# Accumulators of one PSUM bank each in the seven-product stage of an attention and feed-forward kernel

## The chip, the cores and the metric

The kernel runs on one core of a Trainium2 chip. The metric is device time in microseconds of one execution, given as the median of several runs. Engines are named as in the profile: PE (matmul), PEld (weight load), DVE (vector), ACT (scalar), POOL (GpSimd), SP (which issues the output transfers).

## The reference

Block-sparse attention over (4, 8, 768, 64) inputs, then a feed-forward layer over the 3072 tokens:

```python
k_sum = k.reshape(B, H, nb, block, D).max(axis=3)      # block 32
v_sum = v.reshape(B, H, nb, block, D).mean(axis=3)
# each query: keys closer than 16, and the 24 block summaries; softmax over both
x = attn_out.transpose(0, 2, 1, 3).reshape(B * S, H * D)   # 3072 x 512
h = x @ w_in                                               # 512 -> 2048
g = h * (1.0 / (1.0 + np.exp(-beta * h)))
return g @ w_out                                           # 2048 -> 512
```

## The kernel before

The work is cut by batch. Attention of the next batch runs beside the feed-forward layer of the current one; a list of steps with hand-written due times (`run(main, side)`) sets the order in which the instructions are written, and every engine executes its own in that order. Semaphores between the engines are placed by the tile framework: an instruction waits for the earlier instructions that touch the same tile and conflict with it.

The feed-forward layer of one batch has an up part (`h_group`: matmuls into `h_ps`, then a SiLU on ACT into `h_sb`) and a down part. For the first three batches the down part is plain (`o_part`, `o_piece`). For the last batch alone it is done by `down_seven`. There the 768 x 2048 by 2048 x 512 product is treated as a 2 x 2 block matrix product (two halves of tokens, of the 2048 inner columns, and of the 512 output columns) and computed with seven block products in place of eight, as Strassen does. Sums of blocks are formed ahead by DVE (`sums_w`, `sums_h`). This stage is the end of the kernel: nothing but the output transfers comes behind it.

`down_seven` works on three row groups a, b and c (`ms` = 0, 1, 2), each 128 tokens of either half. A product, say a6, is product 6 of group a: eight matmuls of 128 x 256 into half a bank (L690). Each group has three accumulator banks:

- `x` holds products 3 (with 6 added later) and 4,
- `y` holds products 5 and 2,
- `z` holds product 1 (with 7 added later).

Group by group, these readers follow:

- `low_copy` (ACT, L695) copies `y` to SBUF as `o_low`;
- `cross` (DVE, L700 and L701) reads `x` twice;
- `minus` (DVE, L707) reads product 1 in `z`;
- `end(6)` (DVE, L712) reads `x` after product 6 was added, `end(7)` (L712) reads `z` after product 7 was added, and each has SP issue an output transfer (L715). For the last group `cross` issues two transfers as well (L703, L704).

The products of the three groups are written in this order, with the readers behind some of them:

a3 a4 a2 a5 (`a.low_copy`) a1 (`a.cross`, `a.minus`) b3 b4 a6 (`a.end(6)`) a7 (`a.end(7)`) b2 b5 (`b.low_copy`) b1 (`b.cross`, `b.minus`) c5 c2 (`c.low_copy`) c3 c4 (`c.cross`) b6 (`b.end(6)`) b7 (`b.end(7)`) c1 (`c.minus`) c6 (`c.end(6)`) c7 (`c.end(7)`)

PSUM has eight banks. Two are buffers of the small pool (tag `t`); six belong to a pool that can be re-cut: `cut(n)` closes it and opens it anew as 6/n buffers of n banks, and `take(name)` takes the next one. Before the change it stands at n = 2 here. Banks `x` and `z` of a group are the two halves of one tile `o_big`, and `y` is a tile `o_ps` of the small pool.

Of the kernel before, what the change touches and what calls it, by code (L numbers as in the profile page):

```python
# [12 lines left out]
def kernel(  # L13
# [12 lines left out]
    P = 128  # L26
    f32 = mybir.dt.float32
# [19 lines left out]
    d_model = moe_w_in.shape[0]  # L47
# [21 lines left out]
    ps = ctx.enter_context(tc.tile_pool(name="ps", bufs=1, space=bass.MemoryType.PSUM))  # L69
# [209 lines left out]
    def cut(n):  # L279
        if "ctx" in pools:  # L280
            pools.pop("ctx").close()
        pools["ctx"] = ExitStack()
        pools["n"] = n
        pools["pool"] = pools["ctx"].enter_context(tc.tile_pool(name=f"banks{n}", bufs=1, space=bass.MemoryType.PSUM))

    def take(name, dt=f32):
        n = pools["n"]
        return pools["pool"].tile([P, n, 512 if dt == f32 else 1024], dt, name=name, tag="big", bufs=6 // n)
# [383 lines left out]
    class Seven:  # L672
# [2 lines left out]
        def __init__(self, u, ms):  # L675
            self.u, self.ms, self.row = u, ms, units[u][0] * nch + units[u][1] // P + ms

        def open(self):
            big = take("o_big")
            low = ps.tile([P, d_model], f32, name="o_ps", tag="t", bufs=2)  # L680
            n = d_model // 2
            self.x, self.y, self.z, self.n = big[:, 0], low, big[:, 1], n
            self.at = {3: big[:, 0, 0:n], 4: big[:, 0, n:], 5: low[:, 0:n], 2: low[:, n:], 1: big[:, 1, 0:n]}
            self.at[6], self.at[7] = self.at[3], self.at[1]

        def dots(self, *ms):
# [30 lines left out]
    def down_seven(u, add):  # L717
        a, b, c = (Seven(u, ms) for ms in range(HM))
        c.last = u + 1 == len(units)

        def each(z, m, *then):
            def f():
                if m == z.first:
                    z.open()
                z.dots(m)
                for g in then:
                    g()
            add(f)

        for z in (a, b):  # L730
            z.first = 3
        c.first = 5
        for m in (3, 4, 2):
            each(a, m)
        each(a, 5, a.low_copy)
        each(a, 1, a.cross, a.minus)
        each(b, 3)
        each(b, 4)
        each(a, 6, lambda: a.end(6))
        each(a, 7, lambda: a.end(7))  # L740
        each(b, 2)
        each(b, 5, b.low_copy)
        each(b, 1, b.cross, b.minus)
        each(c, 5)
        each(c, 2, c.low_copy)
        each(c, 3)
        each(c, 4, c.cross)
        each(b, 6, lambda: b.end(6))
        each(b, 7, lambda: b.end(7))
        each(c, 1, c.minus)  # L750
        each(c, 6, lambda: c.end(6))
        each(c, 7, lambda: c.end(7))
# [189 lines left out]
    for b in range(B):  # L942
# [6 lines left out]
        main, t = [], 0.0  # L949
# [24 lines left out]
        for u in us_rest:  # L974
            if u in seven:
                def add(f):
                    nonlocal_t[0] = nonlocal_t[0] + OT
                    main.append((nonlocal_t[0] - OT, f))
                nonlocal_t = [t]
                down_seven(u, add)  # L980
                t = nonlocal_t[0]
                continue
            for ms in range(units[u][2] * HM):
                for p in range(4):
                    main.append((t, lambda u=u, ms=ms, p=p: o_part(u, ms, p, 4)))
                    t += OT
# [4 lines left out]
        if b == 0:  # L991
# [23 lines left out]
            for g in pairs:  # L1015
                t = dn0 + OT * TK[g] if g < 2 else up1 + TK[g]
# [15 lines left out]
        elif nxt < B:  # L1032
            for g in pairs:
                t = (2.6, 6.5, 10.4, 14.3)[g]
# [69 lines left out]
```

## Time and profile before

| | |
|---|---|
| median of 3 runs | 211.62 us (211.50 to 212.26) |
| the profiled execution | 213.69 us |
| its span, first to last instruction | 212.0 us |
| PE busy | 202.8 us, 96% |
| DVE busy | 125.7 us, 59% |
| ACT busy | 119.8 us, 57% |
| POOL busy | 83.5 us, 39% |
| mean granted clock of PE | 0.992 |

Times in the trace count from the start of the span. A row of the timeline gives start, time, engine, line, operation, what is written and read, shapes, and the number of instructions merged into the row; in square brackets stands how long the engine had been idle before, and who ended that. Matmuls are pipelined: each of this stage is shown with about 272 ns, while they start closer together than that, so a row of eight ends later than the next row starts.

### The profile page before, as it was taken

What the parts mean: (1) busy time and instruction counts of PE and PEld (TensorE: products, weight loads), DVE (VectorE), ACT (ScalarE), POOL (GpSimd) and SP (SyncE); (2) the same over time, 40 slices, a digit from 0 to 9 for tenths busy, and PEclk for the clock granted to TensorE, in tenths of its full rate; (3) what the DMA queues carried; (4) which work ended last, traced back from release to release, by engine and by line L of the source; (5) the groups of instructions that cost most, each with busy time, mean ns of one, the idle gap of its engine ahead of it and who ended that gap; (6) DMA issues with size and microseconds to landing.
All of it is one profiled execution on the core that took longest, in us unless ns stands there. A gap on an engine that the chain in (4) does not pass through costs nothing.

```text
span 212.0 us, 5108 instructions
## 1 busy us (share of the span) xinstructions
PE 202.8 (96%) x2100; PEld 119.9 (57%) x2100; DVE 125.7 (59%) x339; ACT 119.8 (57%) x172; POOL 83.5 (39%) x122
## 2 busy tenths in 40 slices
PE   7897999999999999999999999999999999999972
PEld 2565655556545555655555456655555566587861
DVE  4884948988969869434626669814435444443341
ACT  3682889159797386668336266678164276631200
POOL 7996999793055399984300094000000000000000
PEclk9996999999999999999999999999999999999999
DMA  6999999999939999999992999900343400000141
GB/s 153 180 156 207 200 205 204 188 151 218 140 62 146 114 202 139 156 163 156 159 216 92 111 179 156 167 13 0 118 108 91 136 2 3 0 0 34 68 148 50
DMA packets 92199, 26.46 MB, mean 125 GB/s; under 512 B 81152, under 2 KB 89360, under 8 KB 92176
## 3 DMA queue, kind: packets, MB, share of 16 engines
q0 software_dynamic: 63888, 13.34, 76.1%
q1 hardware_dynamic: 28080, 12.60, 31.2%
q8 instruction: 16, 0.26, 0.6%
q10 hardware_dynamic: 208, 0.20, 0.3%
q14 instruction: 7, 0.06, 0.1%
HBM read 27.27 MB, written 6.29 MB: 158 GB/s over the span
## 4 chain that ended last, share of the span: by engine, by line
PE 91%; DMA 3%; DVE 2%; issue 2%; POOL 1%; ACT 0%; ACTq 0%
PE h_ps L619 36%; PE o_ps L789 25%; PE o_big L690 5%; PE o_ps L804 5%; PE h_ps L768 4%; DMA q<-in_q_dram 3%; PE av_ps L572 3%; PE o_ps L690 2%; PE s_ps L527 2%; PE px L493 1%; PE s_ps L510 1%; DVE o_two L712 1%; PE vm_ps L376 1%; PE pq L310 1%; PE vm_ps L386 1%
## 5 line engine op out<-in xcount | busy, mean ns | idle before, releaser
L619 PE MATMUL h_ps<-xT,w_in_sb 128*128 128x384 bf16 x464 | 77.1, 327 | 0.0
L632 ACT ACTIVATE h_sb<-h_ps,beta_sb 128x768 bf16<-128x768 f32 (+1 forms) x80 | 59.2, 775 | 23.2 <-PE h_ps L619 19.3
L619 PEld LDWEIGHTS <-w_in_sb 128*128 128x128 bf16 x464 | 45.2, 98 | 30.0 <-issue 0.3
L789 PE MATMUL o_ps<-w_out_sb,h_sb 128*128 128x512 bf16 x240 | 54.9, 380 | 0.0
L789 PEld LDWEIGHTS <-h_sb 128*128 128x128 bf16 x240 | 22.3, 98 | 25.0
L553 DVE TENSOR_TENSOR attn<-attn,band 128x768 bf16<-128x768 bf16 x24 | 13.0, 556 | 18.9 <-ACT attn L502 17.2
L792 ACT COPY o_sb<-o_ps 128x512 f32<-128x512 f32 x15 | 8.9, 596 | 22.3 <-PE o_ps L789 17.1
L112 POOL DMA_DIRECT2D q_all<-in_q_dram x24 | 20.3, 873 | 2.7 <-DMA ve<-in_v_dram 2.7
L502 ACT ACTIVATE attn<-s_ps 128x768 bf16<-128x768 f32 x24 | 17.7, 814 | 3.3 <-PE s_ps L527 2.2
L118 POOL DMA_DIRECT2D ve<-in_v_dram x16 | 16.6, 1051 | 1.8 <-DMA w_out_sb<-in_moe_w_out_dram 1.1
L112 POOL DMA_DIRECT2D k_all<-in_k_dram x16 | 13.9, 883 | 2.8 <-DMA ve<-in_v_dram 2.0
L348 DVE TENSOR_TENSOR half<-kw 128x384 bf16<-128x384 bf16 x16 | 5.8, 365 | 10.8 <-DMA kw<-k_all 10.7
L582 DVE TENSOR_TENSOR x_nat<-av_ps,r 128x768 bf16<-128x768 f32 x12 | 11.5, 958 | 0.5
L690 PEld LDWEIGHTS <-h_sb 128*128 128x128 bf16 x96 | 9.4, 97 | 4.2 <-issue 3.0
L804 PE MATMUL o_ps<-w_out_sb,h_sb 128*128 128x512 bf16 x48 | 11.7, 380 | 0.0
L369 DVE COPY vo<-ve 64x780 bf16<-64x780 bf16 (+3 forms) x28 | 10.6, 380 | 0.6
L665 DVE TENSOR_TENSOR ve<-h_sb 128x768 bf16<-128x768 bf16 x4 | 2.2, 558 | 13.2 <-ACT h_sb L632 13.2
L246 ACT ACT_TABLE_LOAD x7 | 9.0, 1283 | 0.1
L690 PE MATMUL o_big<-w_sum,h_sb 128*128 128x256 bf16 x48 | 6.2, 272 | 2.3 <-DVE o_two L712 1.8
L768 PE MATMUL h_ps<-xT,w_in_sb 128*128 128x384 bf16 x48 | 8.3, 326 | 0.0
L495 ACT COPY xT<-px 128x384 bf16<-128x384 bf16 (+1 forms) x5 | 3.0, 607 | 9.0 <-PE px L493 9.0
L695 ACT COPY o_low<-o_ps 128x512 f32<-128x512 f32 x3 | 1.8, 586 | 10.9 <-PE o_ps L690 10.9
(142 smaller groups left out, 252.8 us busy)
## 6 DMA issues: line engine op xcount, KB each, us to landing
out_dram<-o_sb SPq DMA_DIRECT2D x18, 256.0 KB, 3.1
ve<-in_v_dram POOLq DMA_DIRECT2D x12, 192.0 KB, 6.4
q_all<-in_q_dram POOLq DMA_DIRECT2D x24, 96.0 KB, 6.2
w_in_sb<-in_moe_w_in_dram POOLq DMA_DIRECT2D x8, 256.0 KB, 8.8
k_all<-in_k_dram POOLq DMA_DIRECT2D x16, 96.0 KB, 6.5
w_out_sb<-in_moe_w_out_dram POOLq DMA_DIRECT2D x4, 256.0 KB, 7.0
w_out_sb<-in_moe_w_out_dram POOLq DMA_DIRECT2D x2, 512.0 KB, 9.2
out_dram<-o_two SPq DMA_DIRECT2D x4, 256.0 KB, 2.3
```

The source lines that it names most:

```text
L112: nc.gpsimd.dma_start(out=t[:, :, h], in_=(k_row if nm == "k" else q_row)[b, g, :, h])
L118: nc.gpsimd.dma_start(out=ve_bufs[b % 2][:, lo:hi, 0:D], in_=src)
L369: copy(out=dst, in_=src)
L502: nc.scalar.activation(out=at[(b, g)][:, par].rearrange("p m h f -> p h m f"), in_=sv, func=ACTF.Exp, scale=scale)
L553: nc.vector.tensor_mul(out=a, in0=a, in1=band[:, par])
L582: nc.vector.tensor_mul(out=x.rearrange("p m h d -> p h m d"), in0=ov[:, :, :, 0:D], in1=r[:, :, :, None].to_broadcast([P, 2, n, D]))
L619: nc.tensor.matmul(big[:, j, 0:MG], w_in_sb[:, ki, ni * P:(ni + 1) * P], xT[b][:, ki, tok:tok + MG], start=(ki == 0), stop=(ki == k1 - 1))
L632: nc.scalar.activation(out=hb.rearrange("p (k m) -> p k m", m=MG), in_=big[:, j:j + w, 0:MG], func=ACTF.Silu, scale=beta_sb[:, ni:ni + 1])
L690: nc.tensor.matmul(self.at[m], h[:, c, self.ms * P:(self.ms + 1) * P], w[:, c], start=(c == 0 and m in (1, 3, 2 if self.first == 3 else 5) ...
L768: nc.tensor.matmul(h_open[(u, i)][:, j, 0:MG], w_in_sb[:, ki, ni * P:(ni + 1) * P], xT[b][:, ki, t0 + j * MG:t0 + (j + 1) * MG], start=sta ...
L789: nc.tensor.matmul(o_ps, h_bufs[(u, ni * w // k2)][:, ni % (k2 // w), ms * P:(ms + 1) * P], w_out_sb[:, ni], start=(ni == 0), stop=(ni == ...
L804: nc.tensor.matmul(o_ps, h_bufs[(u, ni * w // k2)][:, ni % (k2 // w), ms * P:(ms + 1) * P], w_out_sb[:, ni], start=(ni == 0), stop=(ni == ...
```

## The change

Each of the accumulators `x`, `y` and `z` becomes a tile of its own, of one bank. At the start of `down_seven`, group a takes both buffers of the small pool as `x` and `y`; the other pool is re-cut into six single banks; a takes one of them as `z`, b takes three, c takes two and uses a's `y` again. The tiles of the re-cut pool are called `o_one`. Lines move up by one from `dots` on: L690 becomes L689, L695 L694, L700 L699, L701 L700, L707 L706, L712 L711, L715 L714.

```diff
-        def open(self):
-            big = take("o_big")
-            low = ps.tile([P, d_model], f32, name="o_ps", tag="t", bufs=2)
+        def open(self, banks):
             n = d_model // 2
-            self.x, self.y, self.z, self.n = big[:, 0], low, big[:, 1], n
-            self.at = {3: big[:, 0, 0:n], 4: big[:, 0, n:], 5: low[:, 0:n], 2: low[:, n:], 1: big[:, 1, 0:n]}
+            x, y, z = banks
+            self.x, self.y, self.n = x, y, n
+            self.at = {3: x[:, 0:n], 4: x[:, n:], 5: y[:, 0:n], 2: y[:, n:], 1: z[:, 0:n]}
             self.at[6], self.at[7] = self.at[3], self.at[1]
...
     def down_seven(u, add):
         a, b, c = (Seven(u, ms) for ms in range(HM))
         c.last = u + 1 == len(units)
+        low = []
+
+        def banks(z):
+            if z is a:
+                low.extend(ps.tile([P, d_model], f32, name="o_ps", tag="t", bufs=2) for _ in range(2))
+                cut(1)
+                return low[0], low[1], take("o_one")[:, 0]
+            if z is b:
+                return tuple(take("o_one")[:, 0] for _ in range(3))
+            return take("o_one")[:, 0], low[1], take("o_one")[:, 0]
 
         def each(z, m, *then):
             def f():
                 if m == z.first:
-                    z.open()
+                    z.open(banks(z))
                 z.dots(m)
```

On PE at the passage from product c1 to c6, near the end of the program, this stands before (`h_sum` is the left operand of product 1, `h_sb` of product 6; the number behind a name tells buffers apart; in brackets, the engine for whose semaphore the instruction waits):

```order
L690 LDWEIGHTS h_sum_1570
L690 MATMUL o_big_3132<-w_sum_1567,h_sum_1570 128x256
L690 LDWEIGHTS h_sb_2850
L690 MATMUL o_big_3132<-w_sum_1567,h_sb_2850 128x256 [waits DVE_49]
L690 LDWEIGHTS h_sb_2850
```

And now, at the same place on PE:

```order
L689 LDWEIGHTS h_sum_1570
L689 MATMUL o_one_3139<-w_sum_1567,h_sum_1570 128x256
L689 LDWEIGHTS h_sb_2850
L689 MATMUL o_one_3138<-w_sum_1567,h_sb_2850 128x256 [waits DVE_49]
L689 LDWEIGHTS h_sb_2850
```

Nothing moved; both products wrote one tile before and write two now. The first matmul of c6 still waits for DVE, but for an earlier instruction of it: the last one that reads `x`.

On DVE the last seven instructions of the stage were these (`c.cross` twice, `b.end(6)` and `b.end(7)` in one row, `c.minus`, `c.end(6)`, `c.end(7)`; names as above, `o_two` is the output tile in SBUF):

```order
L700 TENSOR_TENSOR o_two_3167<-o_big_3132,o_low0_1568 128x512 [waits DMAHW4_49,DMAHW5_49,PE_49,Activation_49]
L701 TENSOR_TENSOR o_low0_1568<-o_big_3132,o_low0_1568 128x256 [waits DVE_49]
L712 TENSOR_TENSOR o_two_3128<-o_big_3065,o_low1_1569 128x256 [waits PE_49] x2
L707 TENSOR_TENSOR o_low0_1568<-o_big_3132,o_low0_1568 128x256 [waits PE_49]
L712 TENSOR_TENSOR o_two_3167<-o_big_3132,o_low0_1568 128x256 [waits DVE_49,PE_49]
L712 TENSOR_TENSOR o_two_3167<-o_big_3132,o_low0_1568 128x256 [waits PE_49]
```

and now they are these:

```order
L699 TENSOR_TENSOR o_two_3173<-o_one_3138,o_low0_1568 128x512 [waits DMAHW4_49,DMAHW5_49,PE_49,Activation_49]
L700 TENSOR_TENSOR o_low0_1568<-o_one_3138,o_low0_1568 128x256 [waits DVE_49]
L711 TENSOR_TENSOR o_two_3134<-o_one_3070,o_low1_1569 128x256 [waits PE_49]
L711 TENSOR_TENSOR o_two_3134<-o_one_3072,o_low1_1569 128x256 [waits PE_49]
L706 TENSOR_TENSOR o_low0_1568<-o_one_3139,o_low0_1568 128x256 [waits PE_49]
L711 TENSOR_TENSOR o_two_3173<-o_one_3138,o_low0_1568 128x256 [waits DVE_49,PE_49]
L711 TENSOR_TENSOR o_two_3173<-o_one_3139,o_low0_1568 128x256 [waits PE_49]
```

The order of the DVE instructions is the same, and each reads a tile of one bank.

## The prediction

> **What bounds the kernel now.** I read the page first, then the waits of the last 25 us, then that stretch in order of time on PE and DVE, and last the output transfers and the clock. The page gives the span and the chain that ended last:
>
> ```profile
> span 212.0 us, 5108 instructions
> PE 91%; DMA 3%; DVE 2%; issue 2%; POOL 1%; ACT 0%; ACTq 0%
> ```
>
> PE carries the chain almost everywhere, so time is only to be had where PE stands still. The change touches nothing ahead of the block products, which start at 187.11 us; I take everything before that as unchanged. In the waits from 187 to 212 us (total, times, longest), PE has two rows:
>
> ```profile
> PE o_big L690 <- DVE o_two L712: 1.8, 3, 0.8
> PE o_big L690 <- DVE o_low L707: 0.5, 1, 0.5
> ```
>
> PE waits four times for a DVE instruction that reads the accumulator. The timeline of PE (start, time, idle before) shows where. Each x8 is one product, each x16 two:
>
> ```profile
> 187.11 1.91 PE L690 MATMUL o_big<-w_out_sb,h_sb 128*128 128x256 bf16 x16
> ...
> 191.48 1.91 PE L690 MATMUL o_big<-w_out_sb,h_sb 128*128 128x256 bf16 x16
> 193.29 1.03 PE L690 MATMUL o_big<-w_sum,h_sb 128*128 128x256 bf16 x8
> 194.83 1.03 PE L690 MATMUL o_big<-w_sum,h_sb 128*128 128x256 bf16 x8 [0.51 <-DVE o_two L712]
> 195.70 1.04 PE L690 MATMUL o_ps<-w_out_sb,ve 128*128 128x256 bf16 x8
> ...
> 200.07 1.91 PE L690 MATMUL o_big<-w_out_sb,h_sb 128*128 128x256 bf16 x16
> 201.82 1.04 PE L690 MATMUL o_big<-w_sum,h_sb 128*128 128x256 bf16 x8
> 203.61 1.03 PE L690 MATMUL o_big<-w_sum,h_sb 128*128 128x256 bf16 x8 [0.75 <-DVE o_two L712]
> 204.48 1.04 PE L690 MATMUL o_big<-w_sum,h_sum 128*128 128x256 bf16 x8
> 206.03 1.03 PE L690 MATMUL o_big<-w_sum,h_sb 128*128 128x256 bf16 x8 [0.51 <-DVE o_low L707]
> 207.58 1.03 PE L690 MATMUL o_big<-w_sum,h_sb 128*128 128x256 bf16 x8 [0.52 <-DVE o_two L712]
> ```
>
> By the order in the code, 193.29 is a6 (row group a, product 6), 194.83 a7, 201.82 b6, 203.61 b7, 204.48 c1, 206.03 c6, 207.58 c7. The idle in brackets understates the loss, because a matmul's modelled end lies beyond the start of the next one. The loss is better read from starts. From 194.83 to 201.82 there are eight products without a stop: 6.99 / 8 = 0.874 us each. That is the pace that PE can hold here.
>
> The DVE timeline says what PE waited for:
>
> ```profile
> 192.48 0.42 DVE L701 TENSOR_TENSOR o_low<-o_big,o_low 128x256 f32<-128x256 f32 x1
> 192.82 0.41 DVE L707 TENSOR_TENSOR o_low<-o_big,o_low 128x256 f32<-128x256 f32 x1
> 194.36 0.42 DVE L712 TENSOR_TENSOR o_two<-o_big,o_low 128x256 f32<-128x256 f32 x1 [1.12 <-PE o_big L690]
> ...
> 202.07 0.69 DVE L700 TENSOR_TENSOR o_two<-o_big,o_low 128x512 f32<-128x512 f32 x1 [2.00 <-issue]
> 202.80 0.42 DVE L701 TENSOR_TENSOR o_low<-o_big,o_low 128x256 f32<-128x256 f32 x1
> 203.14 0.41 DVE L712 TENSOR_TENSOR o_two<-o_big,o_low 128x256 f32<-128x256 f32 x1
> 204.68 0.42 DVE L712 TENSOR_TENSOR o_two<-o_big,o_low 128x256 f32<-128x256 f32 x1 [1.12 <-PE o_big L690]
> 205.55 0.42 DVE L707 TENSOR_TENSOR o_low<-o_big,o_low 128x256 f32<-128x256 f32 x1 [0.45 <-PE o_big L690]
> 207.10 0.42 DVE L712 TENSOR_TENSOR o_two<-o_big,o_low 128x256 f32<-128x256 f32 x1 [1.12 <-PE o_big L690]
> 208.65 0.42 DVE L712 TENSOR_TENSOR o_two<-o_big,o_low 128x256 f32<-128x256 f32 x1 [1.12 <-PE o_big L690]
> ```
>
> a7 (194.83) starts 0.05 us after `a.end(6)` has read product 6 (194.36 + 0.42 = 194.78). But a7 writes `big[:, 1]` and `a.end(6)` reads `big[:, 0]`; they share the tile, not the bank. So with b7 behind `b.end(6)` (203.14 + 0.41 = 203.55), and c7 behind `c.end(6)` (207.52). c6 writes `big[:, 0]` and waits for `c.minus` (205.97), which reads `big[:, 1]`. All four waits come from a tile that is larger than what is read or written.
>
> **The change part by part.** One tile per bank leaves each matmul waiting for the readers of its own bank alone. What that is worth, from the starts:
>
> - a6: two products from 191.48 to 193.29 take 1.81, at pace 1.75; lost 0.06. Before, a6 is behind `a.minus` (192.82 + 0.41 = 193.23). After, it needs only `a.cross`, whose L701 ended at 192.90 in this trace and can only be earlier.
> - a7: 194.83 − 193.29 = 1.54, less 0.874: 0.67. After, it needs `a.minus`, done some 0.9 us before a7 is due at 194.10.
> - b7: 203.61 − 201.82 = 1.79, less 0.874: 0.92. It is the dearest since DVE was in `c.cross` when product 6 came. After, it needs `b.minus`, which follows b1, five products earlier.
> - c6: 206.03 − 204.48 = 1.55, less 0.874: 0.68. After, it needs `c.cross` alone.
> - c7: 207.58 − 206.03 = 1.55: 0.68. After, it needs `c.minus`, and this one is close (below).
>
> Sum: 0.06 + 0.67 + 0.92 + 0.68 + 0.68 = 3.01 us.
>
> Does a new wait take their place? I laid out PE at 0.874 a product: a6 193.23, a7 194.10, then b2, b5, b1, c5, c2, c3, c4 at 200.22, b6 201.09, b7 201.97, c1 202.84, c6 203.72, c7 204.59. A reader starts 1.07 us after the first matmul of its product (207.58 to 208.65). `c.cross` came 1.12 after c4 (second half of the x16 at 200.07, so 200.95, to 202.07): now 201.34, its second step 202.07, then `b.end(6)` at 202.41, `b.end(7)` at 203.04, `c.minus` at 202.84 + 1.07 = 203.91. DVE has gaps between all of these, so its order stays harmless. `c.minus` ends at 204.33; with 0.06 to PE (205.97 to 206.03) c7 could start at 204.39 and is due at 204.59. Cover: 0.20 us. If it is gone, c7 waits by what is missing, at most the 0.68 that it waits now. c6 needs the end of `c.cross`, 202.07 + 0.42 = 202.49, and is due 1.2 us later.
>
> The rest costs nothing. There are as many matmuls, DVE passes, ACT copies and output DMAs as before, in the same order. Group a's first two banks now come from the small pool, the other six from the pool that is re-cut to single banks; its first use is a1, four products after the start, so at about 190.6. The last reader of an `h_ps` bank on ACT ends at 188.21:
>
> ```profile
> 187.31 0.90 ACT L632 ACTIVATE h_sb<-h_ps,beta_sb 128x768 bf16<-128x768 f32 x1 [0.40 <-PE h_ps L619]
> ```
>
> Group c reuses a's bank `y`, as it reused the same buffer before; between a5, after which ACT copies it, and c5 stand eight products, 7 us. A loss from six single-bank buffers filling up is excluded, since a, b and c together take six.
>
> Behind the last matmul come `c.end(7)` on DVE, its DMA issued by SP and the landing. The output transfers now come closer together. SP's issues, the traffic in half-microsecond windows (PE, PEld, DVE, ACT, POOL busy, clock, DMA share, GB/s) and the landing of the `o_two` transfers:
>
> ```profile
> 202.79 0.33 SPq L703 DMA_DIRECT2D out_dram<-o_two  x1
> ...
> 209.10 0.33 SPq L715 DMA_DIRECT2D out_dram<-o_two  x1
> 203.50:204.00 0.50, 0.39 (x4) 0.35 (x4) 0.05 (x1) 0.00 (x0) 0.00 (x0) 1.00 0.69 234
> 204.00:204.50 0.50, 0.50 (x7) 0.44 (x6) 0.00 (x0) 0.00 (x0) 0.00 (x0) 1.00 0.80 268
> 204.50:205.00 0.50, 0.50 (x7) 0.46 (x5) 0.32 (x1) 0.00 (x0) 0.00 (x0) 1.00 0.84 318
> 205.00:205.50 0.50, 0.50 (x5) 0.31 (x4) 0.10 (x1) 0.00 (x0) 0.00 (x0) 1.00 0.61 230
> DMA to landing us min/median/max: 1.7/1.9/3.5
> ```
>
> Bytes flow some 0.7 us after the issue, at a mean of 262 GB/s over these four windows. After the change, `c.cross`'s two transfers of 128 KB and b's two of 256 KB are issued from 202.06 to about 203.5: 0.79 MB, 3.0 us at that rate, so done near 205.8. `c.end(6)` is issued at about 205.25 and its bytes flow from 205.95. So the last two transfers should find a free queue. Bounds: 0, and 3.5 − 1.7 = 1.8 us if the last landing becomes the longest seen. I take 0, since the row is that of a clear queue.
>
> With that, the last reader starts at 204.59 + 1.07 = 205.66 in place of 208.65, its DMA at 206.11 in place of 209.10, and the span ends near 209.0. The profiled execution took 213.69 us, so it would take about 210.7. It is 2.07 us above the median of 211.62, with no sign that this part differs, so I subtract the same 3.01 from the median: **208.6 us**, 1.4% faster.
>
> The Trainium skill, TensorE: Matmul & The Clock Gate, section Back-to-back issue gap, would have it better still: it gives for streams of weight load and matmul about 81 ns each at 128 columns and 131 ns at 512. Between these an estimate for 256 columns is 98 ns, by which the 14 products from a6 on would end 14 × 8 × (109 − 98) = 1.2 us earlier and the sum come to 207.4. The trace does not agree: 0.874 / 8 = 109 ns with nothing in the way, and the measurement decides.
>
> **The rivals.** First, *one wait stays*: c7 behind `c.minus`, with only 0.20 us of cover, or another reader that comes late. It gives back up to 0.68, or 0.92 where it is b7: 209.3 to 209.5. Against it: the steps of 1.07, 0.42 and 0.06 repeat to 0.01 us in the rows.
>
> Second, *the end is handed to the transfers*: landing 1.8 us longer, 210.4. For it: 0.79 MB in 1.5 us of issues, twice as dense as now. Against it: the reckoning above.
>
> Third, *the change does not do what it says*, because PE waits for something other than the shared tile: 211.6, no change. Against it: nothing that DVE writes in these microseconds is read by a7, b7, c6 or c7, so only the accumulator can order them.
>
> Fourth, on the other side, *the clock drops* in a stage that no longer pauses. The windows (columns as above) show that it can drop in this kernel:
>
> ```profile
> 18.00:21.00 3.00, 3.00 (x43) 2.48 (x37) 1.80 (x6) 1.16 (x4) 2.63 (x6) 0.50 1.24 204
> 187.00:193.00 6.00, 6.00 (x56) 5.34 (x55) 3.65 (x8) 1.49 (x2) 0.00 (x0) 1.00 0.00 0
> 203.00:208.00 5.00, 3.36 (x28) 2.72 (x28) 1.83 (x5) 0.00 (x0) 0.00 (x0) 1.00 0.43 157
> ```
>
> At 0.50, 18:21 us loses half of its 3 us, 1.5 us. The gain of 3.0 and the 1.06 us that make 0.5% are gone after 8.1 us at half clock: 212.7 at that point. Against it: the clock was 1.00 both in the six microseconds without a pause and in the five with three pauses. The Trainium skill, same page, section A second HAM failure mode: psum-queue depth-cycling, says that a kernel which cycles through PSUM banks can idle PE so briefly and often that the clock swings between half and full. This change cycles through more single banks; no run so far shows such a swing here, and the four pauses in this trace, which would be its cause, did not set it off.
>
> **How the numbers follow.** Forecast 0.85; one wait stays 0.06; transfers 0.04; no effect 0.03; clock 0.02. What this kernel's measurement can tell from no change is about 0.5%, 1.06 us. Below 210.56 lie the forecast, the one wait and half of the transfers' case: faster 0.93. Same: 0.02 + 0.03 = 0.05. Slower: 0.02. The range's upper end, 209.8, takes in the kept wait (209.5) and a part of a longer landing. The lower, 208.0, is the lowest run (211.50) less 3.01, less 0.5 for the spread of the runs, which was 0.76 from lowest to highest.
>
> **What would show it.** In the profile after, the groups of 8 from 187.11 on should start 0.87 us apart throughout, with no idle before a PE row named after DVE, and the waits of PE on L711 and L706 should be gone; the last DVE read should start near 205.7, `b.end(6)` and `b.end(7)` near 202.4 and 203.0, the span should end near 209.0. A gap before the last x8 would mean that the 0.20 us of cover was not there. A last landing above 2 us would be the transfers; a clock under 1.00 after 187 us the fourth rival. I would be wrong by the whole sum if the four gaps stood where they are.

## The result

The changed kernel took 209.65 us (median of 4 runs, 209.32 to 209.89) beside 211.9 us for the kernel before (4 runs): ratio 0.9893, 95% interval 0.9867 to 0.9919, 2.25 us faster. Measured again on one chip, five runs against 23 of the kernel before, it was 209.29 beside 212.13 us: ratio 0.9864, interval 0.9842 to 0.9885, 2.84 us faster. The forecast was 208.6 us and 3.01 us of gain. In microseconds the first interval is 1.7 to 2.8 and stops short of 3.01; the second, 2.4 to 3.4, holds it.

The chain that ended last, by engine, in the profile after (span 207.6 us, profiled execution 209.32 us), is PE for 96% of the span, where it was 91%:

```profile
span 207.6 us, 5089 instructions
PE 96%; issue 1%; ACT 1%; DVE 0%
```

The PE timeline of the stage after, with the columns of the prediction's:

```profile
185.76 1.91 PE L689 MATMUL o_ps<-w_out_sb,h_sb 128*128 128x256 bf16 x16
...
190.13 1.91 PE L689 MATMUL o_one<-w_out_sb,h_sb 128*128 128x256 bf16 x16
191.87 1.04 PE L689 MATMUL o_ps<-w_sum,h_sb 128*128 128x256 bf16 x8
192.75 1.04 PE L689 MATMUL o_one<-w_sum,h_sb 128*128 128x256 bf16 x8
193.62 1.04 PE L689 MATMUL o_one<-w_out_sb,ve 128*128 128x256 bf16 x8
...
199.73 1.91 PE L689 MATMUL o_one<-w_sum,h_sb 128*128 128x256 bf16 x16
201.48 1.04 PE L689 MATMUL o_one<-w_sum,h_sum 128*128 128x256 bf16 x8
202.35 1.91 PE L689 MATMUL o_one<-w_sum,h_sb 128*128 128x256 bf16 x16
```

No row has an idle in brackets. a6 (191.87) to a7 (192.75) is 0.88, b6 and b7 stand in one row of 16, and so do c6 and c7. The 20 products up to c7 keep the pace of 0.874. On DVE, `b.end(6)`, `b.end(7)`, `c.minus`, `c.end(6)` and `c.end(7)` now are:

```profile
201.06 0.41 DVE L711 TENSOR_TENSOR o_two<-o_one,o_low 128x256 f32<-128x256 f32 x1
201.68 0.42 DVE L711 TENSOR_TENSOR o_two<-o_one,o_low 128x256 f32<-128x256 f32 x1 [0.21 <-PE o_one L689]
202.56 0.42 DVE L706 TENSOR_TENSOR o_low<-o_one,o_low 128x256 f32<-128x256 f32 x1 [0.45 <-PE o_one L689]
203.43 0.42 DVE L711 TENSOR_TENSOR o_two<-o_one,o_low 128x256 f32<-128x256 f32 x1 [0.45 <-PE o_one L689]
204.30 0.42 DVE L711 TENSOR_TENSOR o_two<-o_one,o_low 128x256 f32<-128x256 f32 x1 [0.45 <-PE o_one L689]
```

DVE now waits for PE before each of the last three, by the same 0.45 us, and PE for nobody. From a3 to the last read the stage takes 204.30 − 185.76 = 18.54 us, where it took 208.65 − 187.11 = 21.54: 3.00 less. The spans differ by more, 4.4 us, since the two profiled executions also differ ahead of the stage (last section).

### The profile page after: what moved, and what is told of

It reads as the page before. It is cut to its first block, busy times and chain, and to the rows that moved or that the text cites. A ratio compares the mean times of both kernels' runs of the same rounds, so it can differ in the third digit from the quotient of the medians.

```text
span 207.6 us, 5089 instructions
## 1 busy us (share of the span) xinstructions
PE 200.1 (96%) x2082; PEld 119.7 (58%) x2100; DVE 127.4 (61%) x339; ACT 119.7 (58%) x172; POOL 83.2 (40%) x122
## 4 chain that ended last, share of the span: by engine, by line
PE 96%; issue 1%; ACT 1%; DVE 0%
PE h_ps L619 37%; PE o_ps L798 25%; PE o_one L689 6%; PE o_ps L813 5%; PE h_ps L777 4%; PE o_ps L689 3%; PE av_ps L572 3%; PE w_ps L826 3%; PE s_ps L527 2%; PE pk L310 1%; PE s_ps L422 1%; PE s_ps L510 1%; PE pq L310 1%; PE vm_ps L376 1%; PE px L493 1%
## 5 line engine op out<-in xcount | busy, mean ns | idle before, releaser
L632 ACT ACTIVATE h_sb<-h_ps,beta_sb 128x768 bf16<-128x768 f32 (+1 forms) x80 | 59.2, 774 | 23.3 <-PE h_ps L619 19.4
L798 PE MATMUL o_ps<-w_out_sb,h_sb 128*128 128x512 bf16 x226 | 52.3, 379 | 1.7 <-issue 1.4
L502 ACT ACTIVATE attn<-s_ps 128x768 bf16<-128x768 f32 x24 | 17.7, 814 | 3.3 <-PE s_ps L527 2.2
L813 PE MATMUL o_ps<-w_out_sb,h_sb 128*128 128x512 bf16 x44 | 11.5, 380 | 0.2
L689 PEld LDWEIGHTS <-h_sb 128*128 128x128 bf16 x96 | 9.4, 98 | 1.2
L358 DVE COPY kw<-kw 128x192 bf16<-128x192 bf16 (+2 forms) x32 | 8.1, 298 | 0.0
L255 DVE TENSOR_SCALAR w_out_sb<-w_out_sb,inv_beta 128x512 bf16<-128x512 bf16 x16 | 6.6, 464 | 1.9 <-DMA w_out_sb<-in_moe_w_out_dram 1.9
```

What stands on the lines that cost most here:

```text
L502: nc.scalar.activation(out=at[(b, g)][:, par].rearrange("p m h f -> p h m f"), in_=sv, func=ACTF.Exp, scale=scale)
L632: nc.scalar.activation(out=hb.rearrange("p (k m) -> p k m", m=MG), in_=big[:, j:j + w, 0:MG], func=ACTF.Silu, scale=beta_sb[:, ni:ni + 1])
L689: nc.tensor.matmul(self.at[m], h[:, c, self.ms * P:(self.ms + 1) * P], w[:, c], start=(c == 0 and m in (1, 3, 2 if self.first == 3 else 5) ...
L798: nc.tensor.matmul(o_ps, h_bufs[(u, ni * w // k2)][:, ni % (k2 // w), ms * P:(ms + 1) * P], w_out_sb[:, ni], start=(ni == 0), stop=(ni == ...
L813: nc.tensor.matmul(o_ps, h_bufs[(u, ni * w // k2)][:, ni % (k2 // w), ms * P:(ms + 1) * P], w_out_sb[:, ni], start=(ni == 0), stop=(ni == ...
```

## The experiments

Below, "stage" is the time from the first matmul of a3 to the last DVE read. It is compared, and not the whole time alone, because a stage repeats to 0.01 us while what lies ahead of it varies by some 0.7 us between executions, and by more where the clock fell (last section).

**The two kernels again.** Both unchanged, on one chip.

> The kernel before, unchanged, for a second trace of it. Theory A (the four PE waits are the whole of the change): ratio 1.00, the stage from the first block product to the last DVE read takes 21.54 us again and has the gaps at a7, b7, c6, c7; what lies ahead of the stage is as long as in the changed kernel, so the stage starts near 185.5 us. Theory B (the changed kernel is also a little slower ahead of the stage, which is why the runs gave 2.3 us and not 3.0): the stage starts here 0.7 us earlier than in the changed kernel.

> The changed kernel, unchanged, measured beside the kernel before on the same chip. Theory A: 3.0 us faster, ratio 0.9858, stage 18.54 us. Theory B: 2.3 us faster, ratio 0.989, with the stage still 18.54 us and its start later than in the kernel before.

The kernel before: 212.24 us (12 runs), ratio 1.0004 (0.9979 to 1.0029), stage 208.96 − 187.43 = 21.53 us, with the same gaps. First and last rows of its stage on PE, and the last read on DVE:

```profile
187.43 1.91 PE L690 MATMUL o_big<-w_out_sb,h_sb 128*128 128x256 bf16 x16
...
207.89 1.03 PE L690 MATMUL o_big<-w_sum,h_sb 128*128 128x256 bf16 x8 [0.51 <-DVE o_two L712]
208.96 0.42 DVE L712 TENSOR_TENSOR o_two<-o_big,o_low 128x256 f32<-128x256 f32 x1 [1.12 <-PE o_big L690]
```

The changed kernel: 209.29 us, stage 204.02 − 185.48 = 18.54 us. Its interval, 0.9842 to 0.9885, holds 0.9858 (theory A) and leaves out 0.989 (theory B), though only just. The starts do not support B either. The stage starts at 185.76 and 185.48 in the two traces of the changed kernel. In the traces below where a3 does not wait, it starts at 185.44 to 186.14, and one of these has the tiles of the kernel before (185.69). In its own two traces the kernel before starts the stage late, not early, and not near 185.5 as expected; the last section shows what these two traces have in common. An estimate from the execution with its median time, 212.13 us, does give that start: a span of 210.4, less a stage of 21.54 and 3.35 us behind the last read, is 185.5.

**Group b alone with two banks.** From the changed kernel; the other groups keep single banks. Here and in the next two runs, `two()` takes a tile of two banks and `ones()` a tile of one bank from the re-cut pool, which then holds one of the first kind and four of the second. The cuts show the group in question alone.

```diff
-                return tuple(take("o_one")[:, 0] for _ in range(3))
+                x, zz = two()
+                return x, ones(), zz
```

> The changed kernel, but group b alone keeps x and z in one tile of two banks. Theory A (a wait for each tile of two banks): b7 waits for b.end(6), which DVE reads late behind c.cross, 0.92 us; a7, c6 and c7 do not wait; stage 19.46 us, 0.9 us slower than the changed kernel. Theory C (what matters is the re-cut of the pool or where the banks lie): stage 18.5 us.

Measured: 210.14 us, ratio 0.9902 (0.9877 to 0.9927). On PE, b6, b7 and c1, and on DVE `b.end(6)`, which reads the other bank of b7's tile:

```profile
199.41 1.04 PE L689 MATMUL o_big<-w_sum,h_sb 128*128 128x256 bf16 x8
201.20 1.03 PE L689 MATMUL o_big<-w_sum,h_sb 128*128 128x256 bf16 x8 [0.75 <-DVE o_two L711]
202.07 1.04 PE L689 MATMUL o_one<-w_sum,h_sum 128*128 128x256 bf16 x8
200.74 0.41 DVE L711 TENSOR_TENSOR o_two<-o_big,o_low 128x256 f32<-128x256 f32 x1
```

b7 starts 1.79 us behind b6, so 0.92 lost, 0.05 after the read of the other bank has ended (201.15). Stage 204.90 − 185.44 = 19.46 us, as theory A had it. Theory C has the re-cut of the pool, or the place of the banks, do the work. The first falls here: the pool is re-cut as in the changed kernel, and the wait is back with one tile. The second falls with the tiles of before in another order, further down, whose banks lie where they lay before.

**Group c alone with two banks.** The same edit for c.

```diff
-            return take("o_one")[:, 0], low[1], take("o_one")[:, 0]
+            x, zz = two()
+            return x, low[1], zz
```

> The changed kernel, but group c alone keeps x and z in one tile of two banks. Theory A: c6 waits for c.minus and c7 for c.end(6), 0.68 us each; a7 and b7 do not wait; stage 19.9 us, 1.36 us slower than the changed kernel. Theory C: stage 18.5 us.

Measured: 210.51 us, ratio 0.992 (0.9893 to 0.9946). c1, c6 and c7 on PE:

```profile
201.18 1.04 PE L689 MATMUL o_big<-w_sum,h_sum 128*128 128x256 bf16 x8
202.73 1.03 PE L689 MATMUL o_big<-w_sum,h_sb 128*128 128x256 bf16 x8 [0.51 <-DVE o_low L706]
204.28 1.03 PE L689 MATMUL o_big<-w_sum,h_sb 128*128 128x256 bf16 x8 [0.52 <-DVE o_two L711]
```

Both gaps are back at 1.55 − 0.874 = 0.68 us, stage 205.35 − 185.46 = 19.89 us.

**Group a alone with two banks.** Here a's tile is the first thing that is taken from the re-cut pool; `small()` takes a tile of the small pool. b takes its `y` there too, and c uses a's.

```diff
             if z is a:
-                low.extend(ps.tile([P, d_model], f32, name="o_ps", tag="t", bufs=2) for _ in range(2))
                 cut(1)
-                return low[0], low[1], take("o_one")[:, 0]
+                x, zz = two()
+                low.append(small())
+                return x, low[0], zz
```

> The changed kernel, but group a alone keeps x and z in one tile of two banks. Theory A (a wait for each tile of two banks): a7 waits for a.end(6) again, 0.67 us, and a6 at most 0.06; b7, c6 and c7 do not wait; stage 19.2 to 19.3 us, 0.7 us slower than the changed kernel. Theory C (what matters is the re-cut of the pool or where the banks lie): no gap at a7, stage 18.5 us.

Measured: 211.33 us (12 runs), ratio 0.9968 (0.9944 to 0.9991): 2.0 us slower than the changed kernel, not 0.7. a3, a6 and a7 on PE:

```profile
186.77 1.91 PE L689 MATMUL o_big<-w_out_sb,h_sb 128*128 128x256 bf16 x16 [0.99 <-ACT h_sb L632]
...
191.13 1.91 PE L689 MATMUL o_one<-w_out_sb,h_sb 128*128 128x256 bf16 x16
192.94 1.03 PE L689 MATMUL o_big<-w_sum,h_sb 128*128 128x256 bf16 x8
194.49 1.03 PE L689 MATMUL o_big<-w_sum,h_sb 128*128 128x256 bf16 x8 [0.52 <-DVE o_two L711]
```

a6 and a7 lose 0.06 and 0.68, as expected, and from a3 the stage is 206.04 − 186.77 = 19.27 us. Missed was a wait of 0.99 us ahead of a3, for ACT's last read of an `h_ps` tile. Either the tile of two banks or the pool caused it; the next run separates them.

**Single banks, but a's first one from the re-cut pool.** b takes `y` from the small pool instead.

```diff
             if z is a:
-                low.extend(ps.tile([P, d_model], f32, name="o_ps", tag="t", bufs=2) for _ in range(2))
                 cut(1)
-                return low[0], low[1], take("o_one")[:, 0]
-            if z is b:
-                return tuple(take("o_one")[:, 0] for _ in range(3))
-            return take("o_one")[:, 0], low[1], take("o_one")[:, 0]
+            if z is not c:
+                low.append(ps.tile([P, d_model], f32, name="o_ps", tag="t", bufs=2))
+            return take("o_one")[:, 0], low[0 if z is c else -1], take("o_one")[:, 0]
```

> The changed kernel, but group a takes x from the re-cut pool in place of the small one (all tiles of one bank, six from the re-cut pool as before; b takes y from the small pool). Theory D (the re-cut pool can be used only after ACT has read the last h_ps bank, whichever bank is asked for): a3 waits 1.0 us as in the run where group a kept its tile of two banks, no other gap; stage from a3 18.5 us, the whole 1.0 us slower than the changed kernel. Rival (the wait in that run came from its tile of two banks): no wait, as fast as the changed kernel.

Measured: 210.19 us, ratio 0.9906 (0.9884 to 0.9928). The up part's last matmuls and a3 on PE:

```profile
179.75 5.85 PE L619 MATMUL h_ps<-xT,w_in_sb 128*128 128x384 bf16 x35
186.59 1.91 PE L689 MATMUL o_one<-w_out_sb,h_sb 128*128 128x256 bf16 x16 [0.99 <-ACT h_sb L632]
```

The same 0.99 us, with tiles of one bank and no other gap; stage from a3 205.12 − 186.59 = 18.53 us. Between starts the loss is a little larger: from the first of 35 such matmuls to a3 it is 186.59 − 179.75 = 6.84 us here, and 185.48 − 179.79 = 5.69 in the second trace of the changed kernel, so 1.15 us. It is not the bank that a3 waits for: in the program that this kernel builds, a3's tile lies in bank 2, and the tile that ACT reads last in banks 4 and 5. So closing and re-opening the pool ahead of a3 costs about a third of the gain, unless the first products write elsewhere. The change gives group a both buffers of the small pool first, and that is what hides it.

**The tiles of before, in another order.** From the kernel before; the diff shows what moves.

```diff
         each(a, 6, lambda: a.end(6))
+        each(b, 2)
         each(a, 7, lambda: a.end(7))
-        each(b, 2)
...
-        each(c, 4, c.cross)
+        each(c, 4)
+        each(c, 1, c.cross, c.minus)
         each(b, 6, lambda: b.end(6))
-        each(b, 7, lambda: b.end(7))
-        each(c, 1, c.minus)
         each(c, 6, lambda: c.end(6))
+        each(b, 7, lambda: b.end(7))
         each(c, 7, lambda: c.end(7))
```

> The kernel before, with its tiles of two banks, but its products in another order: a6 b2 a7, and c4 c1 (c.cross, c.minus) b6 c6 b7 c7. Theory A (the tile costs only where the product behind a reader uses the same tile): a7, b7 and c7 have a product of another group between and do not wait; c6 waits for c.minus, 0.87 us, since c.cross is read only behind c1; stage 19.4 us, 2.1 us faster than the kernel before. Theory C (single banks are needed): stage 21.5 us as before.

Measured: 209.83 us, ratio 0.9893 (0.9867 to 0.9919), 2.2 us faster than before with no change to a tile. PE from c1 on:

```profile
199.71 1.04 PE L690 MATMUL o_big<-w_sum,h_sum 128*128 128x256 bf16 x8
200.59 1.04 PE L690 MATMUL o_big<-w_sum,h_sb 128*128 128x256 bf16 x8
202.38 2.78 PE L690 MATMUL o_big<-w_sum,h_sb 128*128 128x256 bf16 x24 [0.76 <-DVE o_low L707]
```

Of the four only c6 waits, 1.79 − 0.874 = 0.92 us (0.87 expected); a7, b7 and c7 follow without a gap. a6 still loses its 0.06. Stage 205.20 − 185.69 = 19.51 us. A shared tile costs nothing where another group's product covers the reader. Single banks, in the old order, take away the rest, 19.51 − 18.54 = 0.97 us.

**The cover of c7 taken away.** From the changed kernel, c6 ahead of c1. In this order `c.end(6)` adds a half of `o_low` that `c.minus` has not formed yet, so those output columns come out wrong; the instructions and their sizes are the same.

```diff
-        each(c, 1, c.minus)
         each(c, 6, lambda: c.end(6))
+        each(c, 1, c.minus)
         each(c, 7, lambda: c.end(7))
```

> The changed kernel with c6 moved ahead of c1, so that c7 follows c1 directly. Theory A (the 0.20 us of cover that c7 has behind c.minus comes from c6 between them): c7 starts 1.55 us behind c1, a loss of 0.68 us, and the stage is 19.2 us. If c7 did not depend on c.minus, 18.5 us.

Measured: 209.94 us, ratio 0.9893 (0.987 to 0.9916). c1 and c7:

```profile
202.73 1.04 PE L689 MATMUL o_one<-w_sum,h_sum 128*128 128x256 bf16 x8
204.28 1.03 PE L689 MATMUL o_one<-w_sum,h_sb 128*128 128x256 bf16 x8 [0.52 <-DVE o_low L706]
```

1.55 us apart, 0.68 lost, stage 205.35 − 186.14 = 19.21 us. So a reader of the same bank still holds PE up, and the product between is the cover.

## Why the prediction was right, and where it was off

- **The sum of the waits**, 3.01 us: the stage became 3.00 and 2.99 us shorter in the two pairs of traces. Each term came back when its group's shared tile did: 0.06 and 0.68 for a, 0.92 for b, 0.68 twice for c.
- **The layout after**: from a3, `b.end(6)`, `b.end(7)` and the last read were put at 15.30, 15.93 and 18.55 us; they came at 15.30, 15.92 and 18.54.
- **The cover of c7**: `c.minus` ends at 202.98, so with 0.06 c7 could start at 203.04; it started 0.87 behind c6, at 203.22. Cover 0.18 us, put at 0.20.
- **"The rest costs nothing"** held, and rested on one choice more than the text made clear: that a1, not a3, is the first use of the re-cut pool. The other choice costs 0.99 us of idle, 1.15 between starts. The row that the prediction shows had the price: ACT's last read ends at 188.21, 1.10 us behind the start of a3.
- **The transfers**: in the changed kernel no landing of an `o_two` transfer took above 2.3 us, and that was one of b's; the last one took 1.7, as before. From the last read to the end of the span it is 3.3 us, where it was 212.0 − 208.65 = 3.35:

```profile
DMA to landing us min/median/max: 1.7/1.9/2.3
```

- **The clock** stayed at 1.00 in the stage in all ten traces, so that rival had nothing for it here. The Trainium skill (TensorE: Matmul & The Clock Gate, A second HAM failure mode: psum-queue depth-cycling) tells of a clock that swings where a kernel cycles through PSUM banks; no run here shows that in this stage.
- **The pace** stayed at 109 ns a matmul, 1.75 us for 16, in a stage without a pause. The estimate of 98 ns from the Trainium skill (TensorE: Matmul & The Clock Gate, Back-to-back issue gap) did not come true.
- **What was off is the base.** The absolute time was 1.05 us too low at first (208.6 for 209.65). The 3.01 were taken from 211.62, a median of three runs; 23 further runs had 212.13, and from that the sum gives 209.12, against 209.29 measured beside them. The rest lies within what varies ahead of the stage. And "no sign that this part differs" was read too quickly: the profiled execution had a stretch at half clock near its start, as a row in the prediction showed, and began the stage 1.35 us later than the one after (187.11 beside 185.76). That is why the span was put near 209.0 and came at 207.6.

## What to carry to other kernels

A wait of PE on a reader is worth looking up by bank: where the two touch different banks, the wait comes from the tile, and either a smaller tile or a product in between removes it. Count such a gap between the starts of two groups against the undisturbed pace, because pipelined rows show only part of it (0.51 for 0.67). A pool that is closed and re-opened made its first user here wait until the old pool's last reader was done (0.99 us of idle); let work that needs other buffers come first.

## What the runs showed of the hardware

Not expected: in two of the ten traces PE's clock was at half for some 3.4 us, each time behind a short pause of PE. At about 16 us the kernel pauses PE for a time that differs between executions. The two traces of the kernel before, and the second of the changed one, on PE behind that pause:

```profile
17.38 0.30 PE L468 MATMUL av_ps<-vd,ablk 128*128 128x65 bf16 x4 [1.53 <-issue]
17.07 0.30 PE L468 MATMUL av_ps<-vd,ablk 128*128 128x65 bf16 x4 [0.85 <-issue]
```

```profile
16.82 0.30 PE L468 MATMUL av_ps<-vd,ablk 128*128 128x65 bf16 x4 [0.54 <-issue]
```

and the windows from 20 to 22 us of the last two (the third number from the end is the clock):

```profile
20.00:22.00 2.00, 2.00 (x10) 1.07 (x8) 1.87 (x18) 0.86 (x3) 1.84 (x4) 0.50 1.24 207
```

```profile
20.00:22.00 2.00, 2.00 (x16) 1.22 (x14) 1.87 (x15) 1.77 (x3) 1.84 (x4) 1.00 1.24 206
```

The clock fell to 0.50 in the two traces with pauses of 1.53 and 0.85 us there, both of the kernel before, and in none of the other eight, whose pause there is 0.70 us at most. It fell some 0.4 and 2.3 us behind the end of the pause, at about 17.7 and 19.4; that the pause is the cause is not shown. These two executions took 213.69 and 213.99 us, 2.07 and 1.75 us above the medians of 211.62 and 212.24, and start the stage at 187.11 and 187.43 in place of 185.4 to 186.1.

What comes ahead of the stage is written the same in both kernels, so I take this for no effect of the change. The runs do not show that: of 47 executions of the kernel before whose mean clock is on record 4 have 0.992 or less, and of 51 of the other kernels none. Four are too few to move the medians compared above. Neither the pauses in the stage, 0.51 to 0.75 us of idle by the rows, nor the one of 0.99 us ahead of a3 set it off: the clock stayed at 1.00 behind them to the end of the stage. So it can be no matter of the pause's length alone. What decides it, the light matmuls around the pause, where it falls in time or something else, stays open.
